# Dilated sliding attention and a gated feed-forward network: residue order 0, 2, 1, 3, finer first loads, a new order of the first units

## The chip, the cores and the metric

The kernel runs on one core of one Trainium2 chip. The metric is the device time of one execution in microseconds (us), lower is better. The core has five engines with queues of their own: TensorE (PE, matrix multiplication and transposes), VectorE (DVE), ScalarE (ACT), GpSimd (POOL, which here mostly issues loads that convert f32 to bf16 on the way) and SyncE (SP, which issues stores and DMA transposes). Each engine takes its instructions in order. Results of PE land in PSUM[...].

## What is computed

Two stages in a row: attention with eight heads, of which heads 0 to 3 have a plain window of 32 and heads 4 to 7 a window of 32 with dilation 4, then a network without biases. Cut to what matters:

```python
q, k, v: (8, 8, 576, 64) f32     # batch, head, sequence, head_dim
scores = q @ k.T / 8
mask_plain = (rel >= 0) & (rel < 32)                        # heads 0 to 3
mask_dil = (rel >= 0) & (rel < 128) & (rel % 4 == 0)        # heads 4 to 7
x = softmax(where(mask, scores, -1e9)) @ v                  # heads side by side: (4608, 512)
out = (((x @ w1) * (x @ w2)) @ w3) @ w_out                  # w1, w2: (512, 1024), w3: (1024, 1024), w_out: (1024, 512)
```

## The kernel before

**Layout.** With dilation 4, tokens of equal residue modulo 4 see only each other. So the dilated heads (the second half of the heads, u = 1) are sorted by residue: four runs of 144 tokens (RUN) follow each other, and in each the window is again a plain band of 32. A batch is cut into six blocks of 96 queries (QB) for each of u = 0 and u = 1, with 32 keys of the block before as a halo. A step is three blocks: four steps for each batch, (u, hf) = (0,0), (0,1), (1,0), (1,1). Half hf = 0 of u = 1 holds the first two residues of the sorted order, hf = 1 the last two. A unit k of the network is half a batch, 288 tokens: unit 2b takes the tokens of the first two residues, 2b+1 those of the last two. Therefore unit 2b needs steps 0, 1 and 2 of its batch, and unit 2b+1 steps 0, 1 and 3.

**Attention.** For each batch q and k are loaded as rows, turned by DVE in 32x32 blocks into `qt` and `kt` (`turn`, tasks T), multiplied on PE (`scores`, tasks S, four banks at a time), put through exp on ACT (`exps`, E), and multiplied with v on PE (`values`, V), with a column of ones for the sum. DVE takes the reciprocal and scales (`recip` R, `norm` N). The result is transposed into `XT`: by PE and a copy for the first two batches (`back` X, `keep` K), by a DMA transpose from SP later (`back_dma`, XD). In batches 0 and 1 the mask is a bias that PE adds through the identity, and v is turned and transposed on the chip (`turn`, `v_back` VT, `v_keep` VK). Later batches multiply with a 0/1 mask on DVE and load v directly into its place. The bias blocks are made by POOL (`band`), ACT (`blocks`) and DVE (`no_halo`). Half u = 0 of batch 0's q and k comes in as f32 on SP and is rounded by ACT (`round_rows`).

**Network.** w3 and w_out are multiplied into one matrix `wf` first: eight pieces, each transposed by PE (`w3_back`, W3T), copied by ACT (`w3_keep`, W3C), multiplied (`w3_mul`, W3M) and put away by DVE (`w3_done`, W3D). Then each unit k has eight tile pairs `A{k}.{f}` and `B{k}.{f}` (`up`, four matmuls of 128x288 each, for w1 and w2). ACT copies A out of PSUM (`copy_a`, CA), DVE multiplies it with B into `gt` (`gate`, G). `down` (Y, eight matmuls of 128x512) makes 128 output tokens, ACT copies them out and SP stores them (`copy_y`, `store`).

**Order.** Nothing is scheduled by hand or on the fly: `Plan` walks a model of the engines before the program is emitted. Each task has a guessed duration, priority and PSUM slots, and the plan's order of start times is the order in which the instructions stand on each engine. So a changed number in the plan can move any instruction. `RANK` orders kinds of task, `ON_DVE` names copies that go to DVE instead of ACT, and `LEAD` says how many batches ahead of the network the scores of a batch may start. Loads stand on POOL in the order in which they are added: after the rows of batch 0 the quarters of w1 and w2 (in two halves of 512 columns each), w_out, six pieces of w3, the rows of batch 1, two pieces of w3. Twelve matmuls on zeros (`warm_up`) run on PE at the start.

Of the kernel before, what the change touches and what calls it, by code (L numbers as in the profile page):

```python
# [10 lines left out]
P = 128  # L11
# [19 lines left out]
TURNED = 2  # L31
ORDER = (2, 3, 0, 1)
RANK = dict(E=1.5, VK=1, K=0.4, N=3, T=1.5, VT=0.2, S=0.3, V=0.1, X=0.4)
WARM = 12
W3_FIRST = 6
SHIFT = {}
ON_DVE = ("K0.0", "K0.2", "K0.3", "K1.2", "VK0.1.0", "VK1.0.1")
GRP = 5
WHOLE = ("qn", "kn")
TURN_LAT = 2700  # L40
LEAD = 1.4
# [13 lines left out]
class Plan:  # L55
# [14 lines left out]
    def run(self):  # L70
# [41 lines left out]
        while len(order) < n:  # L112
            progress = True
            while progress:
                progress = False
                for e in engines:
                    if free[e] > now:
                        continue
                    for r, t in sorted(waiting[e], key=lambda x: x[1].prio):
                        if r > now:  # L120
                            continue
                        at = place(t) if t.slot else 0
                        if at is not None:
                            break
                    else:
                        continue
                    waiting[e].remove((r, t))
                    t.start = now
                    if e == "DMA":
                        free[e] = now + t.dur[0]  # L130
                        dma = max(dma, now + t.dur[0]) + t.dur[1]
                        t.end = dma + 1900
                    else:
                        t.end = free[e] = now + t.dur
                        if t.lat == TURN_LAT and dma > now:
                            t.lat += 3300
                    if t.slot:
                        t.place = at
                        held[at : at + t.slot] = [t] * t.slot
                        if t.slot == 4:  # L140
                            kept = None
                    order.append(t)
                    for u in users[id(t)]:
                        left[id(u)] -= 1
                        if not left[id(u)]:
                            r = max(d.end + (0 if d.eng == u.eng else d.lat) for d in u.deps)
                            waiting[u.eng].append((r, u))
                    progress = True
            ahead = [f for f in free.values() if f > now]
            ahead += [r for e in engines for r, _ in waiting[e] if r > now]  # L150
            ahead += [x for x in map(freed, held) if x is not None and x > now]
            if not ahead:
                left = [t.name for t in self.tasks if t.end is None]
                raise RuntimeError(f"the plan does not end: {left[:20]}")
            now = min(ahead)
# [4 lines left out]
def kernel(  # L160
# [28 lines left out]
    w3_pool = ctx.enter_context(tc.tile_pool(name="w3", bufs=8))  # L189
# [63 lines left out]
    def load_v_dil(b, m):  # L253
        vp = vps[b % 2]
        r, mu = 2 * (m // 3), m % 3
        runs = {
            0: [(0, 96, r, 0)],
            1: [(0, 48, r, 96), (48, 48, r + 1, 0)],
            2: [(0, 96, r + 1, 48)],
        }[mu]  # L260
        for p0, n, res, t0 in runs:
            nc.gpsimd.dma_start(  # L262
                out=vp[32 + p0 : 32 + p0 + n, 4:8, m, 0:D],
                in_=v_rows(b, 4, 4 * t0 + res, [[4 * D, n], [S * D, 4], [1, D]]),
            )
# [5 lines left out]
    def load_w(dst, src, c):  # L271
        f = slice(512 * c, 512 * (c + 1))
        nc.gpsimd.dma_start(
            out=dst[:, :, f], in_=src[:, f].rearrange("(a p) f -> p a f", p=P)
        )
# [32 lines left out]
    def blocks():  # L308

        base = bias[:, 6, :]
        by_res = base.rearrange("p (t r) -> p r t", r=4)
        nc.scalar.copy(
            out=bias[:, 0:4, :].rearrange("p i (r t) -> p i r t", r=4),
            in_=by_res.unsqueeze(1).to_broadcast([P, 4, 4, 24]),
        )
        nc.scalar.copy(out=bias[:, 4, :], in_=base)
        nc.scalar.copy(out=bias[:, 5, 0 : QB // 2], in_=base[:, 0 : QB // 2])
# [17 lines left out]
    def turn(b, u, nm, part):  # L337

        src = qk[(nm, b)][:, u, :].bitcast(U32)
        dst, pad = {"qn": (qts, 0), "kn": (kts, PADK), "vn": (vts, PADK)}[nm]  # L340
        d = dst[b % len(dst)].rearrange("p u w c -> p u (w c)").bitcast(U32)[:, u, :]
        if part is None:
# [3 lines left out]
        n, first, odd = ((5, 0, 2 * RUN + 4), (4, 2 * RUN, 5 - 2 * RUN))[part]  # L346
        o = bass.AP(
            tensor=d.tensor,
            offset=d.offset + pad + first,
            ap=[d.ap[0], [1, n], [RUN, 2], [9, 16], [odd, 2]],  # L350
# [3 lines left out]
            offset=src.offset + part * 64,  # L354
            ap=[src.ap[0], [128, n], [32, 2], [1, 32]],
# [200 lines left out]

    def store(i):
        o_sb = held[("o", i)]
        c0, end = i * P, (i + 1) * P
        at = c0  # L560
        while at < end:
            n = min(end, (at // RUN + 1) * RUN) - at
            b, x = at // S, at % S
            row = b * S + 4 * (x % RUN) + x // RUN
            nc.sync.dma_start(
                out=out[row : row + 4 * (n - 1) + 1 : 4, :], in_=o_sb[at - c0 : at - c0 + n, :]
            )
            at += n
# [9 lines left out]
    def w3_keep(ft):  # L578
        w3T[ft] = wk_pool.tile([P, KFF, P], BF16, tag="w3T", bufs=2, name="w3T")
        nc.scalar.copy(out=w3T[ft], in_=held[("x3", ft)])  # L580
# [13 lines left out]
    def w3_done(ft):  # L594
        nc.vector.tensor_copy(out=wf_sb[:, ft, :], in_=held[("wf", ft)])
# [10 lines left out]
    def first_constants():  # L606
        nc.vector.memset(warm, 0.0)
        nc.vector.memset(bias, 0.0)
# [9 lines left out]
    c0 = add("const", "DVE", 2500, [], first_constants, 0)  # L618
    add("warm", "PE", 1840 + 216 * WARM, [c0], warm_up, 0)
# [29 lines left out]

    def loads_w12(c):  # L650
        return [
            load("LW", 800, 3300, [], lambda d=d, s=s: load_w(d, s, c))
            for d, s in ((w1_sb, moe_w1), (w2_sb, moe_w2))
        ]

    for i, nm in enumerate(WHOLE):
        t = add(f"LF{nm}", "SP", 100, [], lambda nm=nm: load_whole(nm, rows_of[nm], 0), -9 + i,
                lat=4100 + 1350 * i)
# [7 lines left out]
    idt = add("ident", "DMA", (600, 0), [], lambda: make_identity(nc, ident), 2.5, lat=-1900)  # L666
    bnd = add("band", "DMA", (700, 0), [c0], band, 2.6, lat=-1800)
    blk = add("blocks", "ACT", 1200, [bnd], blocks, 0, lat=100)
    blk = add("no halo", "DVE", 150, [blk], no_halo, 0, lat=80)
    mk = add("masks", "DMA", (2500, 0), [blk], masks_of_bias, 26.5, lat=-1800)  # L670
    lw12 = [loads_w12(0), loads_w12(1)]
    for c in range(2):
        lwo[c] = load(f"LWO{c}", 600, 3300, [], lambda c=c: load_wo(c))
    def loads_w3(fts):
        for ft in fts:
            lw3[ft] = load(f"LW3.{ft}", 550, 1400, [], lambda ft=ft: load_w3(ft))

    loads_w3(range(W3_FIRST))
    for nm in ("qn", "kn", "vn"):
        loads_rows(nm, 1)  # L680
    loads_w3(range(W3_FIRST, KFF))

    FUSED, w3m = [], []
    for ft in range(KFF):
        x = add(f"W3T{ft}", "PE", 510, [lw3[ft], idt], lambda f=ft: w3_back(f), 6, slot=1,
                after=[w3m[-2] if len(w3m) > 1 else None])
        y = add("W3C", "ACT", 1012, [x], lambda f=ft: w3_keep(f), -1, lat=100,
                after=[w3m[-2] if len(w3m) > 1 else None])
        z = add(f"W3M{ft}", "PE", 1728, [y, lwo[0], lwo[1]], lambda f=ft: w3_mul(f), 7, slot=1)
        w3m.append(z)  # L690
        FUSED.append(add("W3D", "DVE", 688, [z], lambda f=ft: w3_done(f), -1, lat=100))
# [5 lines left out]
    def turns(b, u, nm, pr):  # L697
        parts = (None,) if u == 0 and nm != "qn" else (0, 1)
        old = last_v.get((b - 1, u)) if nm == "vn" else last_s.get((b - 2, u))
        ts = [  # L700
            add(f"T{nm}{b}.{u}.{part or 0}", "DVE",
                1245 if part is None else 750 if part == 0 else 630, [L[(nm, b, u)], c0],
                lambda part=part: turn(b, u, nm, part), pr, lat=80, after=[old])
# [3 lines left out]
        return ts  # L707

    vals, T = {}, {}
    for b in range(B):  # L710
# [4 lines left out]
        for u in range(2):  # L715
            T[(b, u)] = [
                t for nm in ("kn", "qn") for t in turns(b, u, nm, 10 * b + RANK["T"])
            ]
        for u in range(2):
            if b >= 2:  # L720
                break
            tv = turns(b, u, "vn", 10 * b + RANK["T"])
            for half in range(2):
                x = add(f"VT{b}.{u}.{half}", "PE", 420, tv + [idt],
# [8 lines left out]
        if b >= 2:  # L733
            hal = add(f"HALO{b}", "DVE", 820, LV[b], lambda b=b: halo_v(b), 10 * b + 2, lat=80)
# [5 lines left out]
        def group(blocks, biased):  # L740
# [4 lines left out]
            need = [t for at in sorted({x[0:2] for x in blocks}) for t in T[at]]  # L745
# [33 lines left out]
        while steps < 4 * B:  # L779
# [27 lines left out]
            else:  # L807
                x = add("XD" + n, "SP", 100, ns, st.back_dma, 0, lat=TURN_LAT)
# [7 lines left out]
    def ups(k, f):  # L816
# [3 lines left out]
        wl = lw12[f // 4]  # L820
# [14 lines left out]
    def downs(i):  # L835
# [5 lines left out]
        Y[i] = y  # L841
        cy = add("CY", "ACT", 585, [y], lambda: copy_y(i), -1, lat=100,
# [5 lines left out]
    for k in range(2 * B):  # L848
        for f in range(KFF):
            ups(k, f)  # L850
            if f % 3 == 1 and done < n_y and (done + 1) * P <= k * UNIT:
                downs(done)
                done += 1
# [44 lines left out]
```

## Time and profile before

| | |
|---|---|
| median of three runs | 259.66 us (259.49 to 259.78) |
| the profiled execution, whole time | 260.15 us |
| its span, first to last instruction | 258.4 us |
| mean granted PE clock | 0.985 |
| DVE, ACT, POOL busy | 64%, 48%, 25% |
| up-projections (L516), 1,024 matmuls | 49.0% of the chain of waits |
| down-projections (L543), 288 matmuls | 24.1% |
| PE starts the first up-projection (chain) | 21.33 us |
| PE ends its last matmul | 253.94 us |

The span is what the profiler recorded between the first and last instruction; the whole time has 1.75 us more around it. The chain of waits goes back from the last instruction to what released it, step by step; what is in it set the end of this execution. The granted clock is a share of full speed: 0.5 means that PE's matmuls take twice as long. Busy tenths are given for 40 slices of 6.46 us.

The DMA engines are full for the first half: the slices show a busy share of 0.9 or more from 6.5 us to 129 us, with 200 to 213 GB/s up to 52 us. The other lines stand in the prediction, where they are used.

### The profile page before, as it was taken

What the parts mean: (1) busy time and instruction counts of PE and PEld (TensorE: products, weight loads), DVE (VectorE), ACT (ScalarE), POOL (GpSimd) and SP (SyncE); (2) the same over time, 40 slices, a digit from 0 to 9 for tenths busy, and PEclk for the clock granted to TensorE, in tenths of its full rate; (3) what the DMA queues carried; (4) which work ended last, traced back from release to release, by engine and by line L of the source; (5) the groups of instructions that cost most, each with busy time, mean ns of one, the idle gap of its engine ahead of it and who ended that gap; (6) DMA issues with size and microseconds to landing.
All of it is one profiled execution on the core that took longest, in us unless ns stands there. A gap on an engine that the chain in (4) does not pass through costs nothing.

```text
span 258.4 us, 6741 instructions
## 1 busy us (share of the span) xinstructions
PE 246.9 (96%) x2732; PEld 168.1 (65%) x2732; DVE 166.2 (64%) x338; ACT 122.9 (48%) x211; POOL 65.0 (25%) x101
## 2 busy tenths in 40 slices
PE   6589999999999999999999999999999999999993
PEld 2367865576577676676667766677766766777661
DVE  3966436979898898898858687666654653333220
ACT  4465464493826373453653535636355343333331
POOL 8612476265401728232023050300000000000000
PEclk9689999999999999999999999999999999999999
DMA  7999999999999999999983949652417172211113
GB/s 224 204 206 200 210 213 210 201 90 193 153 177 159 182 186 128 163 184 213 213 89 49 106 56 143 101 75 55 91 39 93 41 91 63 83 39 43 43 41 122
DMA packets 58030, 33.40 MB, mean 129 GB/s; under 512 B 44688, under 2 KB 47760, under 8 KB 58000
## 3 DMA queue, kind: packets, MB, share of 16 engines
q0 software_dynamic: 37488, 18.81, 57.4%
q1 hardware_dynamic: 20512, 14.16, 26.8%
q8 instruction: 21, 0.34, 0.6%
q14 instruction: 9, 0.07, 0.1%
HBM read 38.80 MB, written 9.44 MB: 187 GB/s over the span
## 4 chain that ended last, share of the span: by engine, by line
PE 92%; ACT 2%; DVE 2%; DMA 2%; issue 0%; ACTq 0%; DVEq 0%
PE ps L516 49%; PE ps L543 24%; PE ps L585 5%; PE ps L444 5%; PE ps L408 4%; ACT et L419 2%; PE ps L391 2%; DMA gt<-in_q_dram 2%; PE ps L366 1%; PE ps L573 1%; PE ps L484 1%; DVE qt L357 1%; DVE kt L344 0%; ACT qn L240 0%; DVE vt L344 0%
## 5 line engine op out<-in xcount | busy, mean ns | idle before, releaser
L516 PE MATMUL ps<-XT,w_sb 128*128 128x288 bf16 x1024 | 136.0, 286 | 0.2 <-DVE gt L532 0.2
L516 PEld LDWEIGHTS <-w_sb 128*128 128x128 bf16 x1024 | 97.6, 98 | 30.2 <-issue 0.6
L532 DVE TENSOR_TENSOR gt<-ps,asb 128x288 bf16<-128x288 f32 x128 | 57.9, 454 | 55.2 <-PE ps L516 53.5
L527 ACT CAST asb<-ps 128x288 bf16<-128x288 f32 x128 | 50.9, 398 | 60.5 <-PE ps L516 57.7
L543 PE MATMUL ps<-wf_sb,gt 128*128 128x512 bf16 x288 | 67.7, 379 | 0.0
L554 ACT COPY osb<-ps 128x512 f32<-128x512 f32 x36 | 21.1, 585 | 52.5 <-PE ps L543 52.5
L543 PEld LDWEIGHTS <-gt 128*128 128x128 bf16 x288 | 28.0, 98 | 27.7
L262 POOL DMA_DIRECT2D vp<-in_v_dram x48 | 30.0, 631 | 49.2 <-PE ps L444 16.2
L419 ACT ACTIVATE et<-ps 128x1920 bf16<-128x1920 f32 (+2 forms) x23 | 34.4, 1506 | 5.9 <-PE ps L408 4.7
L467 DVE TENSOR_TENSOR xo<-ps,rcp 96x384 bf16<-96x384 f32 (+1 forms) x48 | 31.8, 678 | 0.6
L357 DVE STREAM_TRANSPOSE qt<-qn 128x320 uint32<-128x320 uint32 (+1 forms) x32 | 21.6, 675 | 3.3 <-ACT qn L240 3.1
L427 DVE TENSOR_TENSOR et<-et,mask 128x960 bf16<-128x960 bf16 (+1 forms) x30 | 18.1, 630 | 3.8 <-ACT et L419 3.6
L444 PEld LDWEIGHTS <-et 128*128 128x128 bf16 x384 | 14.5, 98 | 3.8 <-ACT et L419 1.3
L444 PE MATMUL ps<-vp,et 128*128 128x65 bf16 x384 | 15.6, 195 | 1.0 <-ACT et L419 1.0
L585 PE MATMUL ps<-wo_sb,w3T 128*128 128x512 bf16 x64 | 15.0, 379 | 0.0
L408 PEld LDWEIGHTS <-kt 32*128 32x128 bf16 x768 | 9.5, 95 | 6.1 <-issue 5.6
L357 DVE STREAM_TRANSPOSE kt<-kn 128x320 uint32<-128x320 uint32 (+1 forms) x16 | 10.9, 681 | 3.6 <-PE ps L408 3.5
L408 PE MATMUL ps<-qt,kt 32*128 32x96 bf16 x768 | 12.9, 206 | 0.0
L344 DVE STREAM_TRANSPOSE kt<-kn 128x576 uint32<-128x576 uint32 x8 | 10.0, 1249 | 2.0 <-PE ps L408 2.0
L580 ACT COPY w3T<-ps 128x1024 bf16<-128x1024 bf16 x8 | 8.1, 1012 | 4.8 <-PE ps L573 4.7
L455 DVE RECIPROCAL rcp<-ps 96x12 f32<-96x12 f32 x32 | 6.5, 214 | 5.6 <-PE ps L444 5.5
L248 POOL DMA_DIRECT2D vp<-in_v_dram x6 | 7.3, 1209 | 10.6 <-PE ps L444 10.6
(49 smaller groups left out, 105.4 us busy)
## 6 DMA issues: line engine op xcount, KB each, us to landing
qn<-in_q_dram POOLq DMA_DIRECT2D x7, 576.0 KB, 8.0
kn<-in_k_dram POOLq DMA_DIRECT2D x7, 576.0 KB, 9.0
w_sb<-in_moe_w_dram POOLq DMA_DIRECT2D x4, 512.0 KB, 12.3
w3n<-in_moe_w_dram POOLq DMA_DIRECT2D x8, 256.0 KB, 15.2
out_dram<-osb SPq DMA_DIRECT2D x8, 256.0 KB, 2.8
out_dram<-osb SPq DMA_DIRECT2D x8, 224.0 KB, 2.8
vp<-in_v_dram POOLq DMA_DIRECT2D x6, 288.0 KB, 10.3
out_dram<-osb SPq DMA_DIRECT2D x8, 192.0 KB, 2.6
```

Of the source, the lines that this page charges most:

```text
L262: nc.gpsimd.dma_start(out=vp[32 + p0 : 32 + p0 + n, 4:8, m, 0:D], in_=v_rows(b, 4, 4 * t0 + res, [[4 * D, n], [S * D, 4], [1, D]]),)
L357: nc.vector.transpose(out=o, in_=i)
L408: nc.tensor.matmul(out=self.sp[:, g, QB * i : QB * i + QB], lhsT=kt[prt, u, QB * m : QB * m + P, c], rhs=qq, start=(c == 0 and not biased) ...
L419: nc.scalar.activation(out=ev, in_=self.sp[:, :, 0:x], func=ACT.Exp, scale=scale)
L444: nc.tensor.matmul(out=self.o[:, g, mm, :], lhsT=grp.et[:, c0 : c0 + P], rhs=vps[self.b % 2][:, 4 * self.u + g, 3 * self.hf + mm, 0 : D + ...
L467: nc.vector.tensor_tensor(out=dst, in0=self.o[0:QB, hs, :, 0:D], in1=self.rcp[0:QB, hs, :].unsqueeze(3).to_broadcast([QB, n, 3, D]), op=AL ...
L516: nc.tensor.matmul(out=o, lhsT=w_sb[:, c, f * P : (f + 1) * P], rhs=unit_cols(k, c), start=(j == 0), stop=(j == DCH - 1),)
L527: nc.scalar.copy(out=a_sb, in_=held[("a", k, f)])
L532: nc.vector.tensor_tensor(out=gt[:, f, c0 : c0 + UNIT].rearrange("p (r m t) -> p m r t", r=2, m=BLK), in0=held[("b", k, f)].rearrange("p ( ...
L543: nc.tensor.matmul(out=y, lhsT=gt[:, f, c0 : c0 + P], rhs=wf_sb[:, f, :], start=(f == 0), stop=(f == KFF - 1),)
L554: nc.scalar.copy(out=o_sb, in_=held[("y", i)])
L585: nc.tensor.matmul(out=o, lhsT=w3T[ft][:, g, :], rhs=wo_sb[:, g, :], start=(g == 0), stop=(g == KFF - 1),)
```

## The change

- The four residues are sorted 0, 2, 1, 3 instead of 0, 1, 2, 3 (`RES`); `turn`, `blocks`, `load_v_dil` and `store` follow. The two residues of a half now have the same parity, and the half-turns of u = 1 in batch 0 are cut in four (parts 2 to 5): 2 and 3 serve the even tokens (residues 0 and 2, half hf = 0), 4 and 5 the odd ones. The scores of a step need only the parts of their half.
- w1 and w2 come in pieces of 256, 256 and 512 columns. The order of the loads after batch 0's rows is a list: w3 piece 0, w1 and w2 (three pieces each), q of batch 1, w3 piece 1, k of batch 1, w_out, and so on.
- Units 0 and 1 are interleaved: tiles f = 0 to 3 of both, then f = 4 to 7 of both; no `down` is placed before unit 2.
- The bias is cleared first, the band is made before the identity, and ACT makes the blocks before it rounds q and k.
- W3D goes to ACT except for pieces 3, 4 and 7; `ON_DVE`, `RANK`, `LEAD` and the model's numbers for DMA transposes are changed; w3 has seven buffers instead of eight, w3T three instead of two.
- The last output tile is copied out in two halves of 256 columns, by ACT and DVE, and stored from two queues (`finish`).

The order on PE up to the first up-projections is:

```
before: warm VT0.0.0 VT0.0.1 S0.0 S0.1 V0.0 VT0.1.0 VT0.1.1 S0.2 V0.1 V0.2 X0.0 S0.3 X0.1 X0.2 V0.3 A0.0
after:  warm S0.0 S0.1 VT0.0.0 VT0.0.1 S0.2 V0.0 VT0.1.0 V0.1 X0.0 W3T0 S0.3 V0.2 VT0.1.1 X0.1 X0.2 V0.3 A0.0
```

```diff
-RANK = dict(E=1.5, VK=1, K=0.4, N=3, T=1.5, VT=0.2, S=0.3, V=0.1, X=0.4)
+RES = (0, 2, 1, 3)
+RANK = dict(E=3, VK=1, K=1.5, N=0.4, T=0.4, VT=0.4, S=0.3, V=0.05, X=0.4)
-W3_FIRST = 6
+FIRST_LOADS = ("30", "w0", "w1", "w2", "q1", "31", "k1", "o0", "o1", "32", "33", "34", "v1", "35", "36", "37")
-ON_DVE = ("K0.0", "K0.2", "K0.3", "K1.2", "VK0.1.0", "VK1.0.1")
+ON_DVE = ("K0.0", "K0.1", "K0.2", "K1.1", "K1.2", "K1.3", "VK1.1.0", "W3D3", "W3D4", "W3D7")
-TURN_LAT = 2700
-LEAD = 1.4
+BUSY = 4500
+LEAD = 1.2
...
-        by_res = base.rearrange("p (t r) -> p r t", r=4)
-        nc.scalar.copy(
-            out=bias[:, 0:4, :].rearrange("p i (r t) -> p i r t", r=4),
-            in_=by_res.unsqueeze(1).to_broadcast([P, 4, 4, 24]),
-        )
+        by_res = base.rearrange("p (t h l) -> p l h t", h=2, l=2)
+        for low in range(2):
+            nc.scalar.copy(
+                out=bias[:, 0:4, 48 * low : 48 * low + 48].rearrange("p i (h t) -> p i h t", h=2),
+                in_=by_res[:, low, :, :].unsqueeze(1).to_broadcast([P, 4, 2, 24]),
+            )
...
-        n, first, odd = ((5, 0, 2 * RUN + 4), (4, 2 * RUN, 5 - 2 * RUN))[part]
+        n, first, odd = ((5, 0, RUN + 4), (4, RUN, 5 - RUN))[part % 2]
+        low = max(0, part // 2 - 1)
+        both = 2 if part < 2 else 1
...
+    def finish(i):
...
+        nc.scalar.copy(out=o_sb[:, lo], in_=held[("y", i)][:, lo])
+        nc.vector.tensor_copy(out=o_sb[:, hi], in_=held[("y", i)][:, hi])
+        nc.scalar.dma_start(out=rows[:, lo], in_=o_sb[:, lo])
+        nc.sync.dma_start(out=rows[:, hi], in_=o_sb[:, hi])
...
     def first_constants():
+        nc.vector.memset(bias, 0.0)
         nc.vector.memset(warm, 0.0)
-        nc.vector.memset(bias, 0.0)
+
+    def constants():
...
+    WC = (slice(0, 256), slice(256, 512), slice(512, 1024))
...
-        parts = (None,) if u == 0 and nm != "qn" else (0, 1)
+        if u == 0:
+            parts = (None,) if nm != "qn" else (0, 1)
+        else:
+            parts = (2, 3, 4, 5) if b == 0 else (0, 1)
...
-            need = [t for at in sorted({x[0:2] for x in blocks}) for t in T[at]]
+            need = [t for at in sorted({(x[0], x[1], x[2] // 3) for x in blocks}) for t in T[at]]
...
-        wl = lw12[f // 4]
+        wl = lw12[(0, 0, 1, 1, 2, 2, 2, 2)[f]]
...
-    for k in range(2 * B):
-        for f in range(KFF):
-            ups(k, f)
-            if f % 3 == 1 and done < n_y and (done + 1) * P <= k * UNIT:
-                downs(done)
-                done += 1
+    half = KFF // 2
+    begin = [(k, f + h) for h in (0, half) for k in range(2) for f in range(half)]
+    for k, f in begin + [(k, f) for k in range(2, 2 * B) for f in range(KFF)]:
+        ups(k, f)
+        if k > 1 and f % 3 == 1 and (done + 1) * P <= k * UNIT:
+            downs(done)
+            done += 1
```

## The prediction

> **What bounds the kernel now.** I read the page first. TensorE (PE) is busy for 96% of the span, so a saving has to come from the time in which it idles or runs at half clock, and the slices put that at the two ends.
>
> ```profile
> PE 246.9 (96%) x2732; PEld 168.1 (65%) x2732; DVE 166.2 (64%) x338; ACT 122.9 (48%) x211; POOL 65.0 (25%) x101
> ...
> PE   6589999999999999999999999999999999999993
> ...
> PEclk9689999999999999999999999999999999999999
> ```
>
> Next the list of waits, kept to 60 us onward: PE's only wait there is this one.
>
> ```profile
> PE ps L516 <- DVE gt L532: 0.2, 1, 0.2
> ```
>
> So whatever is ready early in the steady part, PE can gain 0.2 us there at most. Then the chain of waits in order of time (start us, length us, what), for the first 21 us.
>
> ```profile
> 0.73 3.98 DMA gt<-in_q_dram
> ...
> 4.73 1.16 ACT qn L240
> ...
> 5.91 0.76 DVE qt L357
> ...
> 6.69 0.63 DVE qt L357
> 7.33 1.20 DVE kt L344
> 8.53 1.09 DVE vt L344
> ...
> 9.66 1.46 PE ps L366 x12
> 11.12 0.96 PE ps L391 x4
> 12.08 0.60 PE ps L408 x24
> ```
>
> The first rows of q arrive, are rounded on ACT, turned on DVE with k, and then **v** is turned (8.53) before PE does anything: PE's first real work is v's transpose at 9.66, and the first scores end at 12.68. The same scores later take 0.49 + 0.40 instead of 0.96 + 0.60 (chain, 15.80 and 16.29). The windows say why: columns are the stretch, its length, busy time per engine, granted clock, DMA share, GB/s.
>
> ```profile
> 8.00:8.50 0.50, 0.00 (x0) 0.00 (x0) 0.50 (x2) 0.00 (x0) 0.50 (x1) 0.67 1.06 198
> ...
> 14.50:15.00 0.50, 0.50 (x13) 0.50 (x11) 0.00 (x0) 0.50 (x1) 0.45 (x1) 0.51 1.25 209
> ```
>
> A mean of 0.67 puts the drop to half clock at 8.17, and 0.51 the return to full at 14.99. PE did 2.47 us of extra work in between (1.46, 0.96, 0.60, 1.07, 0.60, 0.77 where warm rows of the same work have 0.67, 0.49, 0.40, 0.49, 0.40, 0.54; sum 5.46 against 2.99). From V0.3's end at 21.33 (A0.0, the first up-projection) PE is never idle for long: 0.47 around the four biased score groups of batch 1, 0.2 at 121. Both kernels issue the same 2,732 matmuls, so **the question is how much earlier A0.0 starts**, and whether anything later gives it back.
>
> **The start, step by step.** Durations are those of the rows above or of the groups of instructions. The planned order on PE becomes: warm-up, S0.0, S0.1, VT0.0 (both halves), S0.2, V0.0, VT0.1.0, V0.1, X0.0, W3T0, S0.3, V0.2, VT0.1.1, X0.1, X0.2, V0.3, A0.0.
>
> *Masks before rounding.* ACT now does the blocks' copies ahead of the rounding of q. POOL issues two loads (to 2.46), then the band instead of ident: 0.08 + 0.88 (the span of three selects) ends it at 3.42. ACT needs for 128x384, 128x96, 128x48 steps of 0.45, 0.17, 0.23; two copies of 192 lie at 0.27 each by that slope; 3.47 + 0.94 = 4.41, before q lands at 4.70. Cost 0; it is hidden under the load with 0.3 to spare, and any excess shifts everything. Ident moves to 3.97, the loads of kn and vn behind it by 0.95; those wait in a full queue anyway (kn lands about 10.3 either way, from issue at 3.02 plus its median 7.3).
>
> *S0.0 before VT0.0.* k is turned at 8.53, so S0.0 runs 8.55 to 10.11 at half clock, S0.1 to 11.78. Before, S0.0 ended at 12.68. E0.0 on ACT: 10.16 to 11.29; E0.1: 11.83 to 12.96.
>
> *The clock.* Transitions at 8.17 and 14.99 are 6.82 apart, twice 3.41. In 8.17 to 11.58 PE was busy only from 9.66 (56%) and stayed at half; in 11.58 to 14.99 it was busy throughout and came up. Now PE is busy from 8.55, 89% of the first of these. The Trainium skill, "TensorE: Matmul & The Clock Gate", section "What's actually happening", gives a free-running 3.4 us window, full clock after a busy one and half clock after an idle one. Trace and rule agree on the length, but not on the close: the rule, taken as "no gap over 3.4 us", speaks for no drop in the new kernel (warm-up ends about 5.85, gap 2.7 us); the trace dropped 2.5 us after the last warm-up matmul (5.69 to 8.17), after a window busy for 27%. By the row the new window is busy for 31% and drops too. I take the row for the drop (8.17) and the rule for the return at 11.58.
>
> *ACT is the next queue.* Behind E0.1 ACT holds VK0.0.0, VK0.0.1 (1.50 for two), E0.2, VK0.1.0 (0.80), W3C, E0.3, VK0.1.1; DVE did VK0.1.0 before. That gives 12.97, 14.47, E0.2 to 15.63, VK0.1.0 to 16.43, W3C (1.01) to 17.44, E0.3 to 18.57, VK0.1.1 to 19.4. So an exp is late next, not a turn.
>
> *Finer turns on DVE.* Half-turns of 160 and 128 elements have no row; 320 take 0.73 and 256 take 0.62 (0.68 and 0.57 back to back), so by that slope 0.40 and 0.34; half of the row as the low end, the whole row as the high. After v's turn at 9.62 the first five end at 11.5, in time for S0.2, and all ten that stand ahead of R0.0 at 13.3; R0.0 is due at 14.35. At the high end it would wait until 16.3, 2 us late; I take the slope.
>
> *PE against both.* VT0.0 to 12.45, S0.2 to 13.34, V0.0 waits for VK0.0.0 (13.77) to 14.3, VT0.1.0, V0.1 (VK0.0.1) to 15.2. R0.0 and N0.0 (0.24 + 0.94) end 15.55: X0.0 to 15.86, W3T0 (0.45) to 16.3, S0.3 to 17.2, V0.2 to 17.75, VT0.1.1 to 18.1, X0.1 to 18.35. DVE: two v turns, R0.1, N0.1 to 17.5, K0.0, R0.2, N0.2 (two of 0.55) to 19.2; X0.2 to 19.5, K0.1, K0.2 to 20.1; V0.3 (VK0.1.1) ends 20.05. **A0.0 at 20.15**, against 21.33, and W3T0's 0.45 is already done: 1.18 + 0.45 = **1.63 us**.
>
> **Kept until the end?** *w1, w2 in pieces, units 0 and 1 interleaved.* Landings before, from POOL's waits: w1 and w2 at 14.5, 17.1, 20.2, 22.7. New order at the same pace: w3 piece 13.3, first quarters 14.5 and 15.8, second 17.0 and 18.3, halves 20.9 and 23.9; wanted at 20.15, 22.4 and (after 16 tiles of 0.49) 28.2. Before, the second half was wanted at 25.5 and there at 22.7. Nothing waits in either: 0. Two extra issues of 0.76 on POOL disappear under the full queue. *Loads reordered.* At 2.7 per 576 KB and 1.3 per 256 KB: q of batch 1 at 26.6 (before 38.6), k 30.6, w_out 35.7, v 42.3, last w3 48.9. S1.0 is due after 31 tiles, about 36.1; k's turns end at 36.8 for the second half: no wait. The same 0.47 stays around S1.2 and the tile after S1.3. Adding the w3 phase with its new ACT evictions, I get A2.0 at 61.45 with the same work behind PE as before at 63.18: 1.7 us, so the lead holds. With seven buffers the load of w3's last piece waits for W3T0 (16.3), long before its turn. *Residue order, bufs, W3D on ACT:* same instruction sizes, on engines that the w3 phase does not fill, 0. The stall at 121: -0.2, as its neighbours change.
>
> **Last tile in halves.** Copy before 0.58 (512 columns). ACT 288 columns takes 0.40, DVE 0.45, so halves of 256 about 0.43 on the later engine: -0.15. Its store:
>
> ```profile
> out_dram<-osb SPq DMA_DIRECT2D x8, 256.0 KB, 2.8
> ...
> out_dram<-osb SPq DMA_DIRECT2D x8, 128.0 KB, 2.5
> ```
>
> By the rows each half lands 0.3 sooner, were it alone. The skill's "DMA: Bandwidth & Descriptors", section "Rules for kernel authors", speaks against it: two transfers to disjoint halves share the same 16 engines, so splitting brings nothing: 0.15 in all by the rule, 0.45 by the rows. Both halves are in flight at once here, so I take the middle, -0.3.
>
> **Sum:** 1.63 + 0.2 + 0.3 = 2.13 us. Profiled span 258.4 becomes 256.3; that execution took 260.15 in all and so 258.0; from the median of the runs, 259.66, it is **257.5**.
>
> **Rivals.**
> *The clock returns only at 14.99, as before.* For: a window of 89% has no row. Then VT0.0 ends 13.24, S0.2 14.8, N0.0 16.6, S0.3 18.2, N0.2 20.3, A0.0 21.15: gain 0.63, sum 1.13: 258.5.
> *The clock never drops* (the rule). S0.1 ends 10.36, E0.1 11.75, E0.2 14.4, N0.2 18.1, A0.0 18.95: gain 2.83, sum 3.33: 256.3. Against it: 27% did drop.
> *XT arrives late* (slower). LEAD 1.4 to 1.2 puts a batch's scores nearer to their use. V4.2 now stands 19 tiles (9.3), two Y (3.46), S (0.55) and two V (0.74) ahead of A8.0: 14.1 us, before 19.3; V6.2 the same, V3.2 15.3. What must fit in: R 0.21, N 1.09, the transpose's issue 1.24 and landing 5.2, 7.7 by medians; with the longest issue 2.3 and landing 8.3 it is 11.9, plus a pair of stores ahead on SP (0.84) 12.8. Each us over 14.1 costs two us, over 15.3 three; no gain is left from 15.2 on. At 15.5: 2 x 1.4 + 0.2 = 3.1: 260.6. For it: DVE is 90% busy from 60 to 120. Against: even the maxima fit.
> *Half-turns cost like whole ones, or the masks hold up ACT* by about 2 us: the gain is eaten, 259.5.
>
> **Chances:** forecast 0.47, clock late 0.18, clock kept 0.17, XT late 0.08, turns 0.06; 0.04 for what I don't see, half of it slower. Range 256.2 to 258.9: it takes in both clock cases (0.82) and leaves out the last two. A measurement tells 0.2% (0.52 us) from no change: faster (below 259.14) 0.84, same 0.07, slower 0.09.
>
> **What would show it.** Right: PE's first work after the warm-up at about 8.55 on L391-type matmuls, granted clock back to 1.00 near 11.6, the first up-projection near 20.2, no PE wait over 0.3 us after 60, end of PE near 252. Wrong: the rounding of q starting after 4.8 (masks); R0.0 after 15 (turns); PE waiting for a transposed tile before A8.0 or A12.0 (LEAD); an up-projection waiting on a load of w1 or w2 (pieces).

## The result, and the profile after

| | before | after |
|---|---|---|
| median of six runs, us | 259.72 (259.49 to 260.87) | 257.67 (256.74 to 258.07) |
| ratio, 95% interval | | 0.9907 (0.9881 to 0.9933) |
| the profiled execution: whole time, span | 260.15, 258.4 | 258.07, 256.3 |
| first up-projection starts (chain) | 21.33 | 20.27 |
| PE ends its last matmul (chain) | 253.94 | 252.06 |

The changed kernel is 2.05 us faster; its median is 0.17 us above the forecast of 257.5. PE is busy for 247.0 us with the same 2,732 matmuls, where it was 246.9. The 40 slices of its page (busy tenths of PE, and the granted clock) have the same shape; only the first three have moved.

```profile
PE   7789999999999999999999999999999999999993
...
PEclk9899999999999999999999999999999999999999
```

The chain of waits (start us, length us, what) shows the start as it was forecast in kind: PE goes from k's turn (ends at 8.89) straight into scores (L417), with v's turn beside it on DVE, and exp (L428) follows.

```profile
0.73 4.34 DMA gt<-in_q_dram
...
8.94 0.47 PE ps L417 x23
9.40 0.02 issue
9.43 1.14 ACT et L428
10.56 0.04 issue
10.61 1.44 PE ps L375 x12
12.05 0.96 PE ps L400 x4
```

The first scores end at 9.41 (before 12.68), yet v's transposes (L375) and the bias of the third block's scores (L400) run at half speed: 1.44 and 0.96 us. So the clock drop has not gone; it has moved. The windows give its place (stretch, length, busy time and count of PE, PEld, DVE, ACT, POOL, granted clock, DMA share, GB/s):

```profile
10.00:10.50 0.50, 0.35 (x24) 0.29 (x22) 0.47 (x2) 0.50 (x2) 0.38 (x1) 1.00 1.09 207
10.50:11.00 0.50, 0.39 (x5) 0.39 (x5) 0.50 (x3) 0.50 (x2) 0.00 (x0) 0.50 1.13 201
...
13.50:14.00 0.50, 0.50 (x18) 0.47 (x11) 0.00 (x0) 0.34 (x1) 0.30 (x1) 0.58 1.46 198
```

Half speed from 10.50 to about 13.92 (0.58 is 0.42 us at half and 0.08 at full): 3.42 us where before had 6.82.

The second place is the stall at 121. The waits list had 0.2 us for it. In the chain of before, PE is left at 121.13 for a gate (L532) on DVE and comes back at 121.80, 0.67 us later:

```profile
121.29 0.47 DVE gt L532
...
121.80 1.14 PE ps L516 x8
```

PE's own rows show that not all of this is idle time: PE still issues matmuls that the chain passes by.

```profile
118.02 3.59 PE L516 MATMUL ps<-XT,w_sb 128*128 128x288 bf16 x28
121.80 1.14 PE L516 MATMUL ps<-XT,w_sb 128*128 128x288 bf16 x8 [0.19 <-DVE gt L532]
```

From the start of these 28 matmuls to the start of the next one it is 3.78 us. In the chain of after, 28 of them take 3.43 without a break:

```profile
118.27 3.43 PE ps L525 x28
121.70 1.73 PE ps L552 x8
```

So the stall costs 0.35 us. (The bracket's 0.19 counts from the end of the last matmul, which overlaps the next one in an unbroken row.) Before has a second hole that neither view shows: the 24 up-projections from 204.46 need 3.10 us to the next start, at 3.43 for 28 they would need 2.94, so 0.16 is lost. After has neither, and its list of PE's waits is empty from 60 us to the end.

The end of the same chain shows the two half copies (L573 and L574) behind the last matmul, where before one copy of 0.58 stood:

```profile
252.13 0.38 ACT osb L573
...
252.54 0.42 DVE osb L574
```

DVE's copy waits for ACT's, as its row says:

```profile
252.54 0.42 DVE L574 COPY osb<-ps 128x256 f32<-128x256 f32 x1 [5.10 <-ACT osb L573]
```

From PE's end to the end of the span it is 4.24 us, before 4.46.

For the account of the two profiled executions the starts in PE's rows are used. The chain's 21.33 for before is the end of V0.3; the first up-projection itself was issued at 21.17:

```profile
21.17 1.63 PE L516 MATMUL ps<-XT,w_sb 128*128 128x288 bf16 x12
...
20.27 1.63 PE L525 MATMUL ps<-XT,w_sb 128*128 128x288 bf16 x12 [0.25 <-DVE XT L503]
```

A0.0 0.90 us earlier and W3T0 (0.45) done ahead make 1.35; A2.0 comes at 61.80 in the chain, 1.38 before the point at which before has the same matmuls left (63.18); with the two holes (0.35 and 0.16) it is 1.88 at PE's end (253.94 and 252.06); with the tail (0.22) 2.1.

### The profile page after: what moved, and what is told of

It is laid out like the page before. It is cut to its first block, busy times and chain, and to the rows that moved or that the text cites. A ratio compares the mean times of both kernels' runs of the same rounds, so it can differ in the third digit from the quotient of the medians.

```text
span 256.3 us, 6746 instructions
## 1 busy us (share of the span) xinstructions
PE 247.0 (96%) x2732; PEld 168.5 (66%) x2732; DVE 165.1 (64%) x341; ACT 123.8 (48%) x216; POOL 66.9 (26%) x103
## 4 chain that ended last, share of the span: by engine, by line
PE 91%; DVE 3%; ACT 2%; DMA 2%; issue 0%; DVEq 0%; ACTq 0%
PE ps L525 50%; PE ps L552 24%; PE ps L606 5%; PE ps L453 4%; PE ps L417 4%; DMA gt<-in_q_dram 2%; ACT et L428 1%; PE ps L594 1%; DVE xo L476 1%; PE ps L375 1%; PE ps L400 1%; PE ps L493 1%; DVE qt L366 1%; ACT qn L246 0%; DVE kt L351 0%
## 5 line engine op out<-in xcount | busy, mean ns | idle before, releaser
L563 ACT COPY osb<-ps 128x512 f32<-128x512 f32 x35 | 20.5, 586 | 47.2 <-PE ps L552 47.2
L428 ACT ACTIVATE et<-ps 128x1920 bf16<-128x1920 f32 (+2 forms) x23 | 34.3, 1507 | 5.0 <-PE ps L417 3.4
L366 DVE STREAM_TRANSPOSE qt<-qn 128x320 uint32<-128x320 uint32 (+3 forms) x34 | 22.4, 670 | 2.2 <-ACT qn L246 1.9
L417 PEld LDWEIGHTS <-kt 32*128 32x128 bf16 x768 | 9.3, 93 | 7.4 <-issue 5.2
L417 PE MATMUL ps<-qt,kt 32*128 32x96 bf16 x768 | 12.7, 203 | 1.4 <-DVE kt L351 1.4
L366 DVE STREAM_TRANSPOSE kt<-kn 128x320 uint32<-128x320 uint32 (+3 forms) x18 | 11.6, 642 | 1.9 <-PE ps L417 1.7
L606 PEld LDWEIGHTS <-w3T 128*128 128x128 bf16 x64 | 6.1, 98 | 6.2
```

What stands on the lines that cost most here:

```text
L366: nc.vector.transpose(out=o, in_=i)
L417: nc.tensor.matmul(out=self.sp[:, g, QB * i : QB * i + QB], lhsT=kt[prt, u, QB * m : QB * m + P, c], rhs=qq, start=(c == 0 and not biased) ...
L428: nc.scalar.activation(out=ev, in_=self.sp[:, :, 0:x], func=ACT.Exp, scale=scale)
L563: nc.scalar.copy(out=o_sb, in_=held[("y", i)])
L606: nc.tensor.matmul(out=o, lhsT=w3T[ft][:, g, :], rhs=wo_sb[:, g, :], start=(g == 0), stop=(g == KFF - 1),)
```

## Experiments

Six runs of after fell into two groups: 257.65 to 258.07 us with a mean granted clock of 0.990 to 0.993, and 256.74 and 256.78 with 0.997. So the first question was what the clock at the start is worth; the others are what each part of the change is worth. The median of an experiment depends on how many of its executions fell in which group, so groups are compared.

### Is a late first load, or the clock, the cost of the start?

In after, q's first rows landed at 5.07 instead of 4.70. ACT's load of its function table had moved too, from 0.72 to 1.29 us. A copy that waits for nothing was put ahead of it.

```diff
+    add("table", "ACT", 50, [], lambda: nc.scalar.copy(out=tiny, in_=nc.const_aps.tensor(0.0, [P, 1], F32)), -99)
```

> The changed kernel with one more ACT instruction at the very start, a copy of one constant column that waits for nothing, so that ACT loads its function table at 0.7 us as in the kernel before, not at 1.29 us behind the bias's clearing. In the changed kernel q of batch 0 lands at 5.07 us, in the kernel before at 4.70. Theory A: the later table load shares the DMA engines with q's first packets; then q lands at 4.70 again, its rounding starts at 4.73 instead of 5.09, the first up-projection starts about 0.35 us earlier (19.9 us in a run with the same clock), time 257.3 us. Theory B: the table load has nothing to do with it; rounding at 5.09 as now, time 257.7 us.

The table came back to 0.72, and q still landed at 5.17. Landings in the other profiles of both kernels go from 4.63 to 5.13, so this one is scatter as far as the runs show. The profiled execution (258.27, clock 0.993) dropped like after, at about 10.81; the others took 256.75 to 257.00 with 0.996 to 1.0. The table theory falls.

More warm-up matmuls (`WARM = 16` instead of 12):

> The changed kernel with 16 warm-up matmuls instead of 12. Its six executions so far fall in two groups: two with a granted clock of 0.997 and a span of 255.0 us, four with 0.990 to 0.993 and 255.9 to 256.3. Theory A: which group an execution falls in is set by where the clock's 3.41 us window edges lie against the idle time before k is turned (7.51 to 8.94 us); with four more matmuls that idle time is filled, and every execution is like the faster two: clock 0.996 or more, span about 255.0, time 256.8 us. Theory B: the two groups have another cause; then the spread stays 256.7 to 258.1 us. If the warm-up runs wholly at half clock it ends at 8.4 us and the bias matmuls after it at 9.2 us, 0.3 us late.

256.70 to 257.14, all four with 0.997 or more; A0.0 at 18.89.

The last tile copied and stored whole (`if i == n_y - 1:` made `if i == n_y:`):

> The changed kernel with the last tile copied and stored whole, as before. From the end of PE to the end of the span the kernel before took 4.43 us and the changed one 4.21. If that is the halves' doing, it is 4.4 us again and the time 0.2 us longer (257.9 us). Rival: the end differs by chance of landing; then it stays near 4.2 us.

From PE's end to the span's end 4.4 us (251.0 to 255.4), against 4.24 in after: the halves are worth about 0.2. The other profiles agree: 4.2 to 4.3 in all nine with halves, 4.4 to 4.5 in all five with a whole store. This run also settles the clock's price. Its profiled execution has after's start, q even later at 5.13, but kept the clock: A0.0 at 19.21 against 20.27, so **1.06 us for one window at half speed**.

After again, and 16 warm-ups again, on one chip beside before:

> The changed kernel once more, beside the next two on the same chip. Theory A: two groups again, near 256.8 us where the clock stays up (0.996 or more) and near 257.8 us where it drops for one window (0.990 to 0.993), and nothing between; which one is chance.

> The changed kernel with 16 warm-up matmuls once more. Theory A: all executions at 0.996 or more and 256.7 to 257.2 us, so its median is 0.5 us or more below that of the changed kernel wherever that one falls in the slower group half of the time. Rival: it too falls into the slower group, and the two have the same median.

256.47 to 256.85 and 256.56 to 256.85; before took 259.98 there (ratio 0.9875, 0.986 to 0.9891, for after). No execution dropped, so there was nothing for the warm-up to save. PE's timeline of this execution of after (start, length, what, idle before) is worth a look beside that of the first one. First the dropped one:

```profile
1.53 5.30 PE L628 MATMUL ps<-warm 128*128 128x512 bf16 x12 [1.53 <-DVE warm L632]
6.63 0.88 PE L400 MATMUL ps<-bias,ident 128*128 128x288 bf16 x4
8.94 0.44 PE L417 MATMUL ps<-qt,kt 32*128 32x96 bf16 x24 [1.42 <-DVE kt L351]
```

And the one that kept its clock:

```profile
1.54 4.10 PE L628 MATMUL ps<-warm 128*128 128x512 bf16 x12 [1.54 <-DVE warm L632]
...
8.81 0.44 PE L417 MATMUL ps<-qt,kt 32*128 32x96 bf16 x24 [2.68 <-DVE kt L351]
```

The same twelve matmuls took 5.30 us in one and 4.10 in the other. A full-speed one takes 0.216 (eight in 1.73, the down-projection's rows), so 5.30 is all twelve at half speed, and 4.10 is five to six of them at full. By these lengths the step up came at about 4.3 in the second, and near 7.1 in the first (its bias matmuls still took 0.88 instead of 0.66), in one and the same program, though the page's clock row reads full speed in both. The drop at 10.50 came 3.4 us, one window, behind the step at 7.1; in the run with the table, whose bias matmuls took 1.04, the step was near 7.4 and the drop at 10.81. The execution that idled longer, 2.68 us against 1.42, kept its clock. Nor does PE's busy share in the profile tell them apart. In the window behind the step PE was busy for 54% in after (1.83 of 3.41 us) and 52% (1.78) in the run with the table, and the clock dropped; in the run with the whole store, with the step near 6.8, it was 52% (1.78) too, and no drop came.

Counted over all executions with after's start and 12 warm-ups (after, and the runs with the table and the whole store too): 6 of 19 dropped, at 257.65 to 258.4; 13 kept it, at 256.47 to 257.2. With 16 warm-ups and the same order of the start (these two, and the two with another LEAD and with whole turns below): 0 of 17. But four of the six drops are in the first six executions; on the two chips where both ran, it is 2 of 13 with 12 against 0 of 13 with 16. That is a hint for 16 and no proof, and the next runs show that it isn't a rule.

### Does the old order gain as much from the clock alone?

Before with 20 warm-ups (`WARM = 20`):

> The kernel before with 20 warm-up matmuls instead of 12 and nothing else, which fill PE up to its first work at 9.66 us. Theory A: the half clock from 8.17 to 14.99 us cost it up to 2.47 us of PE time, of which the waits for ACT and DVE hide a part: clock 0.997, first up-projection 1 to 2 us earlier than 21.33, time 257.7 to 258.7 us, so much of the change's gain is the clock's. Theory B: the start is bound by the chain over ACT and DVE and not by PE's speed: clock 0.997 but the up-projections start within 0.3 us of 21.3, time 259.4 us or more.

258.87 (22 runs; ratio 0.9959, 0.9946 to 0.9972). With the clock up, the old order starts A0.0 at 19.82 instead of 21.33 (chain); its executions take 258.6 to 259.2 but for one, the five of 0.990 to 0.992 take 259.4 to 259.9. So the old order can have 1.2 us by eight more warm-ups, most of the time. What the new order gains at an equal clock is beside that: with the clock up, 258.6 to 259.2 stand against 256.47 to 257.2, with one drop 259.4 to 259.9 against 257.65 to 258.4, about 1.8 to 2 us either way. Between this one's span (256.9) and that of after with the clock up (255.1) it is 1.8: A0.0 0.61 earlier (PE's rows, 19.66 and 19.05), W3T0 0.45, the two holes 0.5 (they were there again, at 120 and 206), the tail 0.2.

Before with its 12 warm-ups has two groups as well. Of its 82 executions beside these experiments, 31 had a mean clock of 0.989 to 0.993 (259.47 to 260.14) and 51 of 0.982 to 0.987 (260.03 and more); none kept the clock. The profiled one, with 6.82 us at half speed and 0.985, is of the second group.

Before with the masks made first, ahead of rounding, and 16 warm-ups:

```diff
...
-    bnd = add("band", "DMA", (700, 0), [c0], band, 2.6, lat=-1800)
-    blk = add("blocks", "ACT", 1200, [bnd], blocks, 0, lat=100)
+    bnd = add("band", "DMA", (700, 0), [c1], band, 1.5, lat=150)
+    blk = add("blocks", "ACT", 1200, [bnd], blocks, -5, lat=100)
...
```

> The kernel before with one part of the change: the bias is cleared first, the band is made before the identity and ACT makes the mask blocks before it rounds q and k, so that the plan puts S0.0 ahead of VT0.0; and 16 warm-up matmuls, which keep the clock up. To be read against the kernel before with 20 warm-up matmuls (258.87 us, first up-projection at 19.82 in its profile, clock 0.998). Theory A: the order scores before v's transposes is the start's gain, worth about 0.7 us: first up-projection near 19.1, time 258.1 us. Theory B: without the half-turns the start is bound by the turns on DVE and nothing is gained: 19.8, time 258.8 us.

The first scores came at 8.65, as in the changed kernel, but A0.0 only at 19.97 (clock up; 19.66 with 20 warm-ups alone): PE waits for exp instead (0.39 and 0.77) and for DVE's scaling and copies (0.66 and 0.83). 13 executions with the clock up took 258.8 to 259.6, no better than the last run; 9 dropped, at 260.4 to 261.4. Scores ahead of v are worth nothing in this plan, without the rest of the new order, and 16 warm-ups didn't always hold the clock here.

### The finer turns

Batch 0's half-turns of u = 1 made whole again, plan remade, 16 warm-ups:

```diff
-            parts = (2, 3, 4, 5) if b == 0 else (0, 1)
+            parts = (0, 1)
```

> The changed kernel with 16 warm-up matmuls and the turns of u = 1 in batch 0 in two parts again instead of four, so that a step's scores wait for both halves. To be read against the changed kernel with 16 warm-up matmuls (256.87 us, first up-projection at 18.89, S0.2 at 11.36). Theory A: the turns of q and k for u = 1 then end at about 12.2 instead of 11.5, S0.2's matmuls start 0.3 us later, and the first up-projection moves by no more than that: time 256.9 to 257.2 us. Rival: the start hangs on the DVE chain from there to K0.2; then it moves by 0.8 us or more: 257.7 us.

260.1 (ratio 1.0014, 0.9999 to 1.0029): the whole gain gone. But the plan came out different: X0.3 stands ahead of A0.0, which comes at 20.73 instead of 18.89, and PE waits for an exp twice, ahead of 68.06 and of 104.92. The chain has 2.4 and 1.8 us off PE there; start to start in PE's rows, 1.45 and 0.47 are lost. This run says what the planner makes of the numbers, not what a turn costs. So the turns were made whole with the order of instructions held:

```diff
+        if part > 3:
+            return
+        part = part % 2
```

> The changed kernel with 16 warm-up matmuls and whole turns again for u = 1 of batch 0, but with the order of everything else held: parts 2 and 3 turn all residues, parts 4 and 5 do nothing, and the plan is not made anew. Theory A: e6 was 3 us slower because the plan came out with other holes from 65 us on, not because of the turns; here the turns of q and k end 0.5 us later, R0.0 at 13.5 instead of 13.0, but the two turns of v between N0.0 and R0.1 fall away, so the first up-projection stays within 0.3 us of 18.9 and the time within 0.3 us of 256.87. Rival: the quarters themselves are worth 1 us or more: 258 us.

256.99, and A0.0 at 19.07, against 18.75 in the run with quarters, where q landed 0.1 earlier. The quarters themselves are worth 0.2 us at the start.

### The order of the loads

Nearly the old order of loads in the new kernel, 16 warm-ups:

```diff
-FIRST_LOADS = ("30", "w0", "w1", "w2", "q1", "31", "k1", "o0", "o1", "32", "33", "34", "v1", "35", "36", "37")
+FIRST_LOADS = ("w0", "w1", "w2", "o0", "o1", "30", "31", "32", "33", "34", "35", "q1", "k1", "v1", "36", "37")
```

> The changed kernel with 16 warm-up matmuls and the loads in nearly the old order: w1 and w2 (three pieces each), w_out, six pieces of w3, then batch 1's rows, two pieces of w3. W3T0 then can't fill a wait ahead of the first up-projection. Theory A: that is all that the order of loads brings, 0.45 us: time 257.3 us, no PE wait for a load. Rival: batch 1's rows, which land at 26 to 31 us now and at 38 to 44 us then, are what keeps PE fed; then waits of 1 us or more appear between 30 and 60 us: 258 us or more.

261.54, slower than before (ratio 1.006, 1.0037 to 1.0082). No matmul waits for a load, but DVE does: it stands for 3.80 us until q of batch 1 has landed at 38.2. Batch 1's turns of q and k come late (38 to 49.5 us instead of 30 to 38), and what follows them on DVE (scaling and the copy into `XT`) is late for PE. At 58.90 the chain leaves PE and goes through DVE:

```profile
59.15 1.80 DVE xo L476 x4
60.95 0.74 DVE XT L503 x2
61.69 0.05 issue
61.74 2.13 PE ps L525 x16
```

PE isn't idle for these 2.84 us: its rows have 24 short transposes there, with stops between them that add up to about 2 us, start to start. Behind exp, 0.57 us are lost ahead of 66.36 and 0.47 ahead of 106.40. The rest lies at the start: A0.0 comes at 20.51 instead of 18.89 (q landed 0.3 later here), and without W3T0 done. This kernel was planned anew as well, so the price is that of the order with its plan.

### LEAD

The old `LEAD = 1.4` in the new kernel with 16 warm-ups:

> The changed kernel with 16 warm-up matmuls and LEAD 1.4 instead of 1.2: scores stand 0.2 batch earlier before their use. In the kernel before, PE has a hole of 0.67 us at 121 us (the same at 119.6 in its version with 20 warm-up matmuls); in the changed kernel it is gone. Theory A: the hole comes from where the plan puts score groups beside the gates, and LEAD moves it; with 1.4 it is back: time 257.3 us. Rival: it is another entry of the plan; no hole, time 256.9 us. In neither does PE wait for a transposed tile, so LEAD 1.2 has taken nothing away.

257.35, 0.5 above the same with 1.2 (256.87). A hole is back, ahead of 88.14 instead of 121.80, where PE waits for N (DVE) instead of a gate:

```profile
88.14 1.63 PE L525 MATMUL ps<-XT,w_sb 128*128 128x288 bf16 x12 [0.45 <-DVE xo L476]
```

The eight up-projections before it, from 86.55, take 1.59 us to this start instead of 0.98: 0.61 lost. The other way round, `LEAD = 1.2` and 20 warm-ups in before:

> The kernel before with 20 warm-up matmuls and LEAD 1.2 instead of 1.4. To be read against it with LEAD 1.4 (258.87 us, hole of 0.67 us at 119.6 us, where PE waits for a gate). Theory A: LEAD alone takes the hole away: 258.3 us. Rival: the new plan has another hole somewhere; 258.8 us or more, and the profile shows the place.

With the clock up 258.2 and 258.4, against 258.6 or more for 20 warm-ups alone. Its hole at 120 is gone. The chain has a detour of 1.5 us at 87.5, over the copy of v's halo on DVE, but PE is at work meanwhile:

```profile
87.29 1.67 PE L543 MATMUL ps<-wf_sb,gt 128*128 128x512 bf16 x7
89.02 0.53 PE L444 MATMUL ps<-vp,et 128*128 128x65 bf16 x12
```

Eight down-projections take 1.73 us (the trace has seven of them), which is the time to the next start. No other hole stands between 60 us and the end. So LEAD removes the holes by itself in the old kernel and brings one back in the new one, and both ways the price is near 0.5 us, though on different chips.

## Why the prediction was right, point by point

The sum was met more closely than its terms, and that is luck. It had 1.63 for the start, 0.2 for the stall and 0.3 for the tail, 2.13 in all; the profiles have 1.38 (at A2.0), 0.5 and 0.22, 2.1 in all. The start came out smaller mainly because 21.33 is the end of V0.3; against the issue at 21.17 the forecast of 20.15 is 1.02 earlier, not 1.18.

**Order of scores and v, A0.0 at 20.15.** Measured 20.27, from errors that cancel. The forecast had S0.0 at half clock from 8.55 to 10.11. But its four bias matmuls need no k: they ran behind the warm-up at 6.63 to 7.51, and only 0.47 us of scores was left after k, at full clock. That made E0.0 start at 9.43, not 10.16, although q landed 0.37 late (scatter). ACT was through with v's first two copies at 12.97, not 14.47, so V0.0 never waited for them. Against it the half speed fell on VT0.0 and S0.2 instead of S0.0 and S0.1: S0.2 ended at 13.61, not 13.34. So R0.0, which the forecast had at 14.35 behind a wait for ACT, came at 14.33 behind a slow PE. From there DVE's chain ran as forecast: N0.0 ended at 15.55, as it had, N0.2 at 19.3 (19.2).

**The clock.** Size right, place wrong, and this is the step that could have missed. I took the drop from the row (8.17) and the return from the rule (11.58), one window at half speed. It was one window, at 10.50 to 13.92. And it is not one answer: the rival "never drops" (A0.0 18.95, 256.3) is what 13 of 19 executions did (19.05, 256.47 to 257.2). What failed is taking the windows' place (8.17, 11.58) from one execution of before. The Trainium skill, "TensorE: Matmul & The Clock Gate", section "What's actually happening", calls the window free-running and the number of slow matmuls at the start different from run to run; here it differs by five to six (5.30 against 4.10), and I used the window's length but not that it has no fixed place. The range held both, and that the median of six fell in the slower group, by four to two, is luck too: in the four of the repeat it would have been 256.75.

**Finer turns.** 160 elements took 0.46 us, 128 took 0.41 (groups of instructions); the ten ahead of R0.0 ran from 9.80 to 13.36, 0.36 each, where 13.3 was forecast: the slope, not the high end.

```profile
L366 DVE STREAM_TRANSPOSE qt<-qn 128x160 uint32<-128x160 uint32 x2 | 0.9, 457 | 0.0
...
L366 DVE STREAM_TRANSPOSE qt<-qn 128x128 uint32<-128x128 uint32 x2 | 0.8, 405 | 0.0
```

**Masks.** ACT's copies ended at 4.16 (forecast 4.41), before q: nothing.

**Pieces of w1 and w2, loads.** No up-projection waited for a load, as said. But "0" for the order of loads hides that the old order with this plan costs over 4 us (261.54 against 256.87): it isn't free, it carries the plan.

**The stall at 121.** Mis-sized: 0.2 was taken from the waits list; it was 0.35, and the hole of 0.16 behind 204 was not seen. Together they are the 0.5 gained between A2.0 and PE's end.

**The tail.** 0.22 against 0.3 forecast, but not by the forecast's way. The two copies didn't run side by side: both write one tile, and DVE's began at 252.54, behind ACT's end at 252.51. So the last copy ended 0.90 after PE, before 0.65: 0.25 lost where 0.15 was to be won. From there to the end of the span it is 3.34 instead of 3.81: 0.47 won, more than the rows' 0.3. That does not fit the rule that the forecast quoted from the Trainium skill, "DMA: Bandwidth & Descriptors" (section "Rules for kernel authors"; its row on halves speaks of partitions, these are halves of the columns); but the halves were issued at 252.53 and 252.99, so no run shows two that start together. Copies into two tiles were not tried.

**XT late.** Never seen: no wait of PE for XT after 60 us, neither in after nor in its repeats. In the sum for this rival, 2 x 1.4 + 0.2 is 3.0, not 3.1; in the list of loads, the last piece of w3 comes at 46.2 by the pace used there, not 48.9. Nothing hangs on either.

## What to carry to other kernels

Where a program starts with warm-up matmuls, look at several executions, not one: whether the clock drops between warm-up and first work can differ, and a change of order that also fills that gap is credited with the clock's gain. A hole's size is to be read from the engine's own rows, start to start, against the same work elsewhere. The chain gave 0.67 us for a hole of 0.35 and 1.5 for none at all, because the engine works on while the chain runs through another; the list of waits gave 0.2, and missed a second one. And an order of loads can cost without PE ever waiting for a load, through the helper engine that gets to the loaded rows later.

## What was not expected of the hardware

That the windows of the clock lie elsewhere in each execution (down and up at 10.50 and 13.92 in one, 10.81 and about 14.22 in another, 8.17 and 14.99 in before) is in keeping with the free-running window of the page named above; that it splits the executions of one kernel into two groups 1.1 us apart is what I had not expected. What decides a drop stays open: before dropped after a window busy for 27%; after dropped at 10.50 after one busy for 54%, the run with the table after 52%, while the run with the whole store kept full speed after 52%, and the repeat after 2.68 us of idling without a break. The Trainium skill, "TensorE: Matmul & The Clock Gate", section "What's actually happening", has the drop after an idle window; by these records a partly busy one is enough at times. Half speed at the start cost 1.06 us here; the two groups lie 1.6 to 1.7 apart in the runs with whole turns and with the masks first, and why more there was not traced.

Not run alone were the residue order, the interleaving of the first units and W3D on ACT: each changes the plan as a whole, so their own shares stay open. What of the 0.6 to 0.9 us at A0.0 is due to which part of the new order of the start stays open too; scores first by themselves brought nothing, and the finer turns 0.2.
